# Row counts of DMA transfers in a long convolution: 52 to 50, whole to 100 and 28, and 117 and 11 to whole

## The chip, the cores and the metric

The kernel runs on one core of a Trainium2 chip. The metric is the device time of one execution in microseconds (us). The engines are TensorE (PE; PEld are its weight loads), VectorE (DVE), ScalarE (ACT), GpSimd (POOL) and SyncE (SP), which only issues DMAs. ACT issues some DMAs too. All transfers run on the core's 16 DMA engines.

## The reference

A causal convolution over the sequence by FFT, followed by a gated projection. x is 8 x 6400 x 128, h is 6400 x 128, all float32.

```
def _attn_ref(x, h):                       # S = 6400, L = 2 * S
    Xf = np.fft.rfft(x, n=L, axis=1)
    Hf = np.fft.rfft(h, n=L, axis=0)
    y = np.fft.irfft(Xf * Hf[None, :, :], n=L, axis=1)[:, :S, :]

def _moe_ref(x, w_val, conv_w, w_out):     # x is y of above, K = 5
    for k in range(K):
        gate_pre += conv_w[k][None, None, :] * xp[:, k:k + S, :]
    gate = 1.0 / (1.0 + np.exp(-gate_pre))
    return gate * (x @ w_val) @ w_out
```

## The kernel before, in words

The sequence is factored as 100 x 64 (N1, N2), and the transform goes through TensorE in four stages, each a set of matmuls with constant tables.

- **Stage 1** (`Forward`): an x tile holds 4 channels of both halves; `load` brings it in as two half tiles of 52 rows (constant TR; 50 of the rows, HR, are used by the matmuls), at partitions 0 and 64. The first three tiles of each batch (and the first eight of the kernel) come as one transfer of 128 rows. `sums` makes sums and differences (tile sd), `half` does the 16 matmuls per tile and half, and two ACT copies write gy.
- **Stage 2** (`Product`): 13 blocks, each with a table block of m2 (128 rows of 4,096 bytes) and a block of the spectrum of h, hd. Both come into a ring: three m2 places and four hd places, 4,096 bytes a row each.
- **Stage 3** (`s3_quads`): 16 steps g per batch. A step does a quad of stage 3 on PE, and in the same step stage 1 of the next batch (`fx.half`, `fx.sums`, which also loads the next x tile), the loads of ring blocks for the coming stage 2 (`ahead`, issued by ACT, by the table AHEAD of step to block), and for chunks of the batch the value projection, gating, output projection and store (tables VALUE and OUTPUT of chunk to step; nine chunks are stored in stage 3). In the first batch, steps 0 to 7 also load pieces of the table m4 (`m4_load`).
- **Stage 4** (`s4`, `copies`, `taps`): interleaved with stage 2 of the next batch.

The **head** is stage 1 of h and of the first x, then stage 2 of both together. Its first six m2 blocks come through `spread`, which cuts a transfer at row KR = 117 into one of 117 rows and one of 11.

The order on every engine is the program's order (`_InOrder`). SP issues DMAs in that order, and stands at one whose semaphores are not there yet; so does ACT. The DMAs of SP and ACT together use eight completion semaphores (DMAHW0 to 7) in turn.

Everything is issued by one wrapper, so that all instructions of the profile have line L122; groups are told apart by their tiles: x (x tiles), sd, gy and gh (stage 1 out), pt (PSUM), ring (the ring, and stage 4 values that live in it), m_sb (table m4, and in the head x tiles and m2 blocks that use its place), yl, gl, p (stage 4), xl, hl, m, hd, out (DRAM).

Of the kernel before, what the change touches and what calls it, by code (L numbers as in the profile page):

```python
# [16 lines left out]
C = 128  # L17
# [3 lines left out]
HR = N1 // 2  # L21
HP = 64
MW = 3 * HR
M4H = 4
SB = 4
# [14 lines left out]
M2B = 3  # L40
MH = 6
HB = 4
XB = 3
XH = 8
TR = 52
M2_AT = (14, 19, 24, 27, 29)
KR = 117
VALUE = {10: 0, 15: 1, 20: 2, 25: 4, 30: 5, 35: 6, 40: 8, 45: 10, 50: 12, 55: 14}
OUTPUT = {10: 2, 15: 3, 20: 4, 25: 6, 30: 7, 35: 8, 40: 9, 45: 11, 50: 13}
ORDER = (60, 0, 35, 40, 45, 50, 55, 5, 10, 25, 15, 20, 30)  # L50
KEEP = {0: 1, 5: 3, 10: 1, 15: 2, 20: 3}
AHEAD = {
    2: (1, 0, 0), 3: (1, 0, 1), 4: (0, 0, 0), 5: (0, 0, 1), 7: (1, 1, 0), 8: (0, 1, 0),
    9: (0, 1, 1), 10: (0, 2, 0), 11: (0, 2, 1), 12: (1, 1, 1), 13: (1, 2, 0), 14: (1, 2, 1),
}

# [78 lines left out]
def longconv_moe(ctx: ExitStack, tc: tile.TileContext, x, h, r1, m2, r3, m4, w64, out):  # L135
    nc = _Engines(tc)
# [15 lines left out]
    m4_sb = cp.tile([128, N2 + 2, MW], F32, name="m4_sb")  # L152
# [8 lines left out]
    m2_sb = [r.rearrange("p (s a c) -> p s a c", a=2, c=C) for r in ring_at[:M2B]]  # L161
    h_sb = [ring_at[M2B + i] for i in (2, 0, 1, 3)]
# [10 lines left out]
    hd = dp.tile([NKB, 128, 2 * SB * C], F32, name="hd")  # L173
# [74 lines left out]
    class Forward:  # L248
# [6 lines left out]
        def load(self, n=1):  # L255
            whole = len(self.xs) == XH and self.o == 0
            for _ in range(n):
                if self.n < NS:
                    t, v = self.xs[self.n % len(self.xs)], self.src[self.n]
                    if whole and self.n < XH or n > 1:  # L260
                        nc.sync.dma_start(t, v)
                    else:
                        for r in (0, HP):
                            nc.sync.dma_start(t[r : r + TR], v[r : r + TR])
                    self.n += 1

        def sums(self, e, sub=nc.gpsimd):
# [32 lines left out]
    def count(kb):  # L300
        return min(SB, HR - kb * SB)

    m4_flat = m4_sb.rearrange("p n t -> p (n t)")
    m2_head = m2_sb + [
        m4_flat[:, i * 2 * SB * C : (i + 1) * 2 * SB * C].rearrange("p (s a c) -> p s a c", a=2, c=C)
        for i in range(M2B, MH)
    ]

    def m2_load(kb, ms=m2_sb, dma=nc.sync.dma_start):
        if kb < NKB:  # L310
            n = count(kb)
            dma(ms[kb % len(ms)][:, :n], m2[:, kb * SB : kb * SB + n])

    def h_load(kb):
        if kb < NKB:
# [1 line left out]
            nc.sync.dma_start(h_sb[kb % HB][:, :n], hd[kb, :, :n])  # L317

    def ahead(spectrum, kb, half):
        i = half * SB // 2  # L320
        if spectrum:
            k = slice(2 * C * i, 2 * C * i + SB * C)
            nc.scalar.dma_start(h_sb[kb % HB][:, k], hd[kb, :, k])
        else:
            j = kb * SB + i
            nc.scalar.dma_start(m2_sb[kb % M2B][:, i : i + SB // 2], m2[:, j : j + SB // 2])

    def laid(t, kb):
        n = count(kb)
# [22 lines left out]
    class Spectrum:  # L352
# [7 lines left out]
        def store(self):  # L360
            n = 2 * count(self.kb) * C
            nc.sync.dma_start(hd[self.kb, :, :n], self.h[:, :n])
# [83 lines left out]
    class Chunk:  # L446
# [119 lines left out]
                        self.o[k * HP : (k + 1) * HP, i : i + o.shape[1]], lhsT=w, rhs=o, start=True, stop=True  # L566
                    )

        def store(self, y=None):
            y = self.y if y is None else y  # L570
            act(y, self.o)
            i, k = _out_range(self.ch)
            nc.sync.dma_start(out[self.b, i:k].rearrange("(e n t) -> e n t", e=C, n=self.ch[1]), y)

# [14 lines left out]
    for g, (f, i) in enumerate(order):  # L591
        e = f.half()
        if g + 2 < 2 * NS:
            order[g + 2][0].sums(nc.vector, nc.vector)
        if g in M2_AT:
            m2_load(M2_AT.index(g), m2_head, spread)
        if NS - len(xh) <= g < NS:
            fx.load()
        e[0](act)
        e[1](act)  # L600
    next(wgen)
    for kb in range(len(M2_AT), MH):
        m2_load(kb, m2_head, spread)
    nc.sync.dma_start(r3_sb, r3)

    def m4_load(j, half=None):
        a = CH * j, CH * j + CH + (j == 12)
        if half is not None:
            a = (a[0] + 2 * half, a[1] if half else a[0] + 2)
        a = slice(*a)  # L610
        nc.sync.dma_start(m4_sb[:, a], m4.rearrange("k (n t) -> k n t", t=MW)[:, a])

    m4_rest = [12, 7, 5, 8, 4, 9, 10, 11, 6]
    sp, pr = {0: Spectrum(0)}, {}
# [25 lines left out]
    for b in range(B):  # L640
        nxt = b + 1 < B


        steps = collections.defaultdict(list)
        for c in pend:
            a = c.ch[0]
            if a == HEAD[0]:
                t = NS - 1
            else:
                t = VALUE[a]  # L650
            if c.late:
                k = (a - WAIT) // CH
                if not nxt:
                    c.r = rows[k % 3]
                steps[2 * k] += [lambda c=c: c.taps(range(2))]
                steps[2 * k + 1] += [lambda c=c: c.taps(range(2, 4)), c.add]
            steps[t] += [c.project]
            steps[t if a in OUTPUT else NS - 1] += [c.sigm, c.gate]
            if a in OUTPUT:
                steps[OUTPUT[a]] += [c.output]  # L660
                steps[OUTPUT[a] + 1] += [c.store]
        pend = [c for c in pend if c.ch[0] in (HEAD[0], HEAD[0] - CH)]
        for g in range(NS):
            e = s3_quads(4 * g)
            f = []
            if nxt:
                f = fx.half([single(), single()])
                fx.sums(nc.gpsimd)
            for u in e:
                u()  # L670
            if nxt and g in AHEAD:
                ahead(*AHEAD[g])
            for u in f:
                u(act)
            if b == 0:
                next(wgen, None)
                next(wgen, None)
                if g < 8:
                    m4_load(m4_rest[0], g % 2)
                    if g % 2:  # L680
                        m4_rest.pop(0)
            for u in steps[g]:
                u()
        if nxt:
            h_load(HB - 1)
        if b + 2 < B:
            fx = Forward(x[b + 2], gy)


        chs = CHUNKS if not nxt else [(a, CH) if a < HEAD[0] else HEAD for a in ORDER]  # L690
        cs = [Chunk(b, i, ch, nxt) for i, ch in enumerate(chs)]
        jobs = collections.defaultdict(list)
        for i, c in enumerate(cs):
            if i and not c.late and not c.held:
                jobs[i + 3].append(c)
        if not nxt:
            jobs[NCH + 2].append(cs[0])
        pr = {}

        def s2(kb):  # L700
            if nxt and kb < NKB:
                pr[kb] = Product(kb)
                m2_load(kb + M2B)

        def times(kb):
            if kb in pr:
                pr[kb].mul_u()
                pr[kb].mul_t()
                pr.pop(kb).add()
                h_load(kb + HB)  # L710

        outs, at = [], 0
        for s in range(max(NCH, *jobs) + 2):
            kbs = list(range(at, min(at + 2 - s % 2, NKB))) if nxt else []
            at += len(kbs)
            if s == 0:
                s2(0)
                s2(1)
            if s < 2:
                cs[s].s4()  # L720
            late = pend[s : s + 1]
            if late and s == 0:
                late[0].output()
            for kb in kbs[:1]:
                if kb:
                    s2(kb + 1)
            if m4_rest:
                m4_load(m4_rest.pop(0))
            for c in jobs[s]:
                c.project()  # L730
            if 1 < s < NCH:
                cs[s].s4()
            for c in outs + late[: s]:
                c.output()
            for c in jobs[s]:
                c.sigm()
            for kb in kbs[:1]:
                times(kb)
            for kb in kbs[1:]:
                s2(kb + 1)  # L740
            if s < NCH:
                cs[s].copies()
            for c in outs + late:
                c.store(p_t[0][:, : c.ch[1]] if s == 0 or nxt and c.ch[0] == CH else None)
            for kb in kbs[1:]:
                times(kb)
            if 0 < s <= NCH and not cs[s - 1].late:
                cs[s - 1].taps()
            for c in cs[1:]:
                if not c.late and s == c.i + (3 if c.held and c.ch[0] == HELD else 2):  # L750
                    c.add()
            for c in jobs[s]:
                c.gate()
            outs = jobs[s]
            if b + 2 < B:
                if s == 5:
                    fx.load(XB)
                if s in (10, 11):
                    fx.sums(nc.gpsimd)
        pend = [cs[0]] + [c for c in cs if c.held or c.late]  # L760
# [45 lines left out]
```

## Time and profile before

| | us |
|---|---|
| median of 3 runs | 935.6 |
| lowest, highest | 933.1, 936.11 |
| profiled execution | 933.86 |
| its span, first to last instruction | 932.0 |
| PE busy | 855.5 |
| DVE busy | 744.5 |
| POOL busy | 560.4 |
| ACT busy | 515.7 |

The profile is of one execution, whose own time of 933.86 us stands beside its span; 1.86 us lie around the span. Busy times are of engines that work side by side, so they don't add up. A wait is idle time of an engine ahead of an instruction, put down to the event that ended it.

The span falls into the head's stage 1 (0 to 45 us), its stage 2 (45 to 95), the third stage of the first batch (95 to 145), then in turn stages 4 and 2 (some 52 us) and stage 3 (some 54 us) of each further batch, and the last batch's end from 832 us on.

### The profile page before, as it was taken

To read this page: it belongs to the slowest core of one execution; us is meant where nothing else is said; L and a number is where in the kernel's file an instruction comes from. 1 tells how busy PE (TensorE), PEld (TensorE's weight loads), DVE (VectorE), ACT (ScalarE), POOL (GpSimd) and SP (SyncE) were. 2 spreads that over 40 slices of the span, in tenths; PEclk is the share of its full clock that TensorE was granted. 3 is DMA by queue.
4 is the path that set the end of the run, shared out by engine and by line. 5 is a ranking of instruction groups with operands and counts; after the bars stand their busy time and mean duration, and the time that the engine had idled before them with its cause. 6 is when DMAs were issued, how large, how long until landed. Compare 5 with 4: busy or idle time off the path is not lost. (4 is left out here: it accounts for less than half of the span.)

```text
span 932.0 us, 48248 instructions
## 1 busy us (share of the span) xinstructions
PE 855.5 (92%) x21360; PEld 683.5 (73%) x21360; DVE 744.5 (80%) x1057; ACT 515.7 (55%) x1238; POOL 560.4 (60%) x570
## 2 busy tenths in 40 slices
PE   6799668999999999999999999999999989999897
PEld 6699668965699558976689567985689657984563
DVE  5456657888887978888797978888897887978786
ACT  6532452277624874177623875167723785258776
POOL 0046644786477864877477855877558763765333
PEclk9899889999999999999999999999999999999999
DMA  7786647926594456925585465925586364921112
GB/s 241 228 294 225 188 140 238 339 67 185 171 312 154 147 175 204 317 70 172 164 298 180 127 189 171 329 87 167 176 275 223 107 181 159 326 78 48 67 57 99
DMA packets 77847, 171.80 MB, mean 184 GB/s; under 512 B 15246, under 2 KB 28558, under 8 KB 77638
## 3 DMA queue, kind: packets, MB, share of 16 engines
q1 hardware_dynamic: 65542, 146.68, 47.0%
q10 hardware_dynamic: 12096, 22.03, 8.2%
q8 instruction: 168, 2.75, 1.3%
q14 instruction: 41, 0.34, 0.1%
HBM read 135.90 MB, written 32.77 MB: 181 GB/s over the span
## 5 line engine op out<-in xcount | busy, mean ns | idle before, releaser
L122 POOL TENSOR_TENSOR gy<-gy,ring 128x512 f32<-128x512 f32 (+1 forms) x182 | 220.4, 1240 | 103.9 <-DVE ring L122 52.6
L122 PEld LDWEIGHTS pt<-r_sb,gy 64*64 64x64 f32 x8192 | 143.2, 138 | 108.1 <-issue 73.9
L122 PEld LDWEIGHTS pt<-m_sb,dt 128*64 128x64 f32 x4096 | 184.8, 136 | 24.0 <-issue 10.6
L122 DVE TENSOR_TENSOR dt<-pt,ring 128x496 f32<-128x496 f32 x256 | 159.6, 665 | 47.2 <-ACT dt L122 45.9
L122 PE MATMUL pt<-m_sb,dt 128*64 128x100 f32 x4096 | 191.4, 248 | 4.3 <-DVE ring L122 2.9
L122 PE MATMUL pt<-gy,ring 128*64 128x128 f32 x3008 | 187.6, 278 | 8.2 <-PE pt L122 3.1
L122 ACT COPY ring<-pt 128x512 f32<-128x512 f32 (+2 forms) x216 | 128.2, 601 | 116.6 <-PE pt L122 48.8
L122 POOL TENSOR_TENSOR sd<-x 128x256 f32<-128x256 f32 x224 | 179.6, 831 | 17.9 <-issue 13.3
L122 PEld LDWEIGHTS pt<-gy,ring 128*64 128x64 f32 x3008 | 174.7, 135 | 20.3 <-PE pt L122 8.0
L122 PE MATMUL pt<-r_sb,gy 64*64 64x64 f32 x8192 | 162.6, 226 | 19.9 <-issue 14.2
L122 PE MATMUL pt<-r_sb,sd 50*64 50x100 f32 x4608 | 141.0, 260 | 25.7 <-issue 18.6
L122 DVE TENSOR_TENSOR gy<-pt,ring 128x1024 f32<-128x1024 f32 (+1 forms) x99 | 117.0, 1182 | 55.5 <-PE pt L122 53.7
L122 PEld LDWEIGHTS pt<-r_sb,sd 50*64 50x64 f32 x4608 | 119.0, 142 | 31.8 <-issue 21.9
L122 DVE TENSOR_TENSOR ring<-pt,ring 128x1024 f32<-128x1024 f32 (+2 forms) x131 | 134.6, 1027 | 7.0
L122 ACT COPY gy<-pt 128x400 f32<-128x400 f32 x256 | 113.5, 503 | 30.8 <-PE pt L122 24.9
L122 ACT COPY yl<-pt 128x500 f32<-128x500 f32 (+1 forms) x89 | 51.2, 575 | 125.9 <-PE pt L122 125.8
L122 POOL TENSOR_TENSOR gl<-gl,p 128x500 f32<-128x500 f32 (+1 forms) x46 | 54.1, 1177 | 101.9 <-DVE gl L122 50.8
L122 ACT COPY dt<-pt 128x16 f32<-128x16 f32 (+3 forms) x318 | 65.3, 265 | 67.5 <-PE pt L122 67.5
L122 DVE SCALAR_TENSOR_TENSOR gl<-yl,w_sb,gl 128x500 f32<-128x500 f32 (+1 forms) x107 | 94.1, 884 | 3.3 <-ACT gl L122 1.2
L122 PE MATMUL pt<-ring,w_sb 128*64 128x500 f32 x320 | 82.6, 602 | 10.0 <-DVE ring L122 9.2
L122 DVE SCALAR_TENSOR_TENSOR ring<-pt,w_sb,ring 128x500 f32<-128x500 f32 (+3 forms) x94 | 63.2, 672 | 11.8 <-ACT ring L122 7.4
L122 POOL TENSOR_TENSOR gy<-gy,m_sb 128x512 f32<-128x512 f32 x24 | 30.4, 1286 | 65.4 <-DVE m_sb L122 65.4
(59 smaller groups left out, 765.7 us busy)
## 6 DMA issues: line engine op xcount, KB each, us to landing
ring<-m SPq DMA_DIRECT2D x66, 512.0 KB
ring<-hd SPq DMA_DIRECT2D x63, 512.0 KB
x<-xl SPq DMA_DIRECT2D x194, 104.0 KB
ring<-hd ACTq DMA_DIRECT2D x42, 256.0 KB
ring<-m ACTq DMA_DIRECT2D x42, 256.0 KB
out<-ring SPq DMA_DIRECT2D x40, 250.0 KB
out<-yl SPq DMA_DIRECT2D x40, 250.0 KB
x<-xl SPq DMA_DIRECT2D x21, 256.0 KB
```

Source lines behind the costliest of these rows:

```text
L122: return self._tc.keep_in_program_order(call(*args, **kwargs))
```

## The change: row counts of transfers

- x half tiles have 50 rows (HR) instead of 52.
- `spread` now cuts at row 100 (KR), into 100 and 28 rows. It is used for the nine stores of a third stage and for the pieces of m4 in the first batch's third stage, which were transfers of 128 rows.
- The ring blocks that ACT loads in stage 3 were two halves by columns (128 rows of 2,048 bytes); now they are 100 and 28 rows of 4,096 bytes. The two loads of m2 block 0 move from steps 4 and 5 to 5 and 6.
- The head's six m2 blocks come in one transfer of 128 rows each.

```diff
-TR = 52
-KR = 117
+KR = 100
 AHEAD = {
-    2: (1, 0, 0), 3: (1, 0, 1), 4: (0, 0, 0), 5: (0, 0, 1), 7: (1, 1, 0), 8: (0, 1, 0),
+    2: (1, 0, 0), 3: (1, 0, 1), 5: (0, 0, 0), 6: (0, 0, 1), 7: (1, 1, 0), 8: (0, 1, 0),
...
                         for r in (0, HP):
-                            nc.sync.dma_start(t[r : r + TR], v[r : r + TR])
+                            nc.sync.dma_start(t[r : r + HR], v[r : r + HR])
...
     def ahead(spectrum, kb, half):
-        i = half * SB // 2
+        r = slice(KR, 128) if half else slice(0, KR)
         if spectrum:
-            k = slice(2 * C * i, 2 * C * i + SB * C)
-            nc.scalar.dma_start(h_sb[kb % HB][:, k], hd[kb, :, k])
+            nc.scalar.dma_start(h_sb[kb % HB][r], hd[kb, r])
         else:
-            j = kb * SB + i
-            nc.scalar.dma_start(m2_sb[kb % M2B][:, i : i + SB // 2], m2[:, j : j + SB // 2])
+            nc.scalar.dma_start(m2_sb[kb % M2B][r], m2[r, kb * SB : kb * SB + SB])
...
         if g in M2_AT:
-            m2_load(M2_AT.index(g), m2_head, spread)
+            m2_load(M2_AT.index(g), m2_head)
...
-                steps[OUTPUT[a] + 1] += [c.store]
+                steps[OUTPUT[a] + 1] += [lambda c=c: c.store(dma=spread)]
...
-                    m4_load(m4_rest[0], g % 2)
+                    m4_load(m4_rest[0], g % 2, spread)
```

The instructions of PE, DVE and POOL stand in the same order as before; only DMA rows differ.

On SP, in the third stage of the second batch, where x half tiles and outputs alternate (in brackets the semaphores waited for: DMAHW are earlier DMAs, Pool is GpSimd's sums, Activation the copy that makes the output), before:

```order
L122 DMA x_83<-xl 52x512 [waits DMAHW2_49,Pool_49]
L122 DMA x_83<-xl 52x512 [waits DMAHW3_49]
L122 DMA out<-ring 128x500 [waits DMAHW4_49,Activation_49]
L122 DMA x_81<-xl 52x512 [waits DMAHW5_49,Pool_49]
L122 DMA x_81<-xl 52x512 [waits DMAHW6_49]
L122 DMA out<-ring 128x500 [waits DMAHW0_49,DVE_49,Activation_49]
L122 DMA x_82<-xl 52x512 [waits DMAHW1_49,Pool_49]
```

and now:

```order
L121 DMA x_83<-xl 50x512 [waits DMAHW4_49,Pool_49]
L121 DMA x_83<-xl 50x512 [waits DMAHW5_49]
L121 DMA out<-ring 100x500 [waits DMAHW6_49,Activation_49]
L121 DMA out<-ring 28x500 [waits DMAHW7_49]
L121 DMA x_81<-xl 50x512 [waits DMAHW0_49,Pool_49]
L121 DMA x_81<-xl 50x512 [waits DMAHW1_49]
L121 DMA out<-ring 100x500 [waits DMAHW2_49,DVE_49,Activation_49]
L121 DMA out<-ring 28x500 [waits DMAHW3_49]
L121 DMA x_82<-xl 50x512 [waits DMAHW5_49,Pool_49]
```

Each output is two transfers, the x half tiles keep their place, and the eight semaphores come round sooner.

On ACT, in the third stage of the first batch, steps 3 to 5 (the copies feed gy, which stage 2 of the next batch reads), before:

```order
L122 DMA ring<-hd 128x512 [waits DMAHW3_49]
L122 COPY gy<-pt_1592 128x400 [waits PE_49]
L122 COPY gy<-pt_1593 128x400
L122 COPY ring<-pt_1625 128x32x2x8 [waits DVE_49,PE_49,Activation_49]
L122 COPY dt<-pt_1625 128x4x4 x2
L122 DMA ring<-m 128x512 [waits DMAHW7_49,DMAHW0_49]
L122 COPY gy<-pt_1658 128x400 [waits PE_49]
L122 COPY gy<-pt_1659 128x400
```

and now:

```order
L121 DMA ring<-hd 28x1024 [waits DMAHW6_49]
L121 COPY gy<-pt_1589 128x400 [waits PE_49]
L121 COPY gy<-pt_1590 128x400
L121 COPY ring<-pt_1623 128x32x2x8 [waits DVE_49,PE_49,Activation_49]
L121 COPY dt<-pt_1623 128x4x4 x2
L121 COPY gy<-pt_1656 128x400 [waits PE_49]
L121 COPY gy<-pt_1657 128x400
L121 COPY ring<-pt_1689 128x32x2x8 [waits DVE_49,PE_49,Activation_49]
L121 COPY dt<-pt_1689 128x4x4 x2
L121 DMA ring<-m 100x1024 [waits DMAHW2_49]
```

The ring loads stand between the same copies, the first m2 load one step later, and each still waits for an earlier DMA's semaphore.

## Rows read from the trace of the kernel before

**Rows 1.** The page: busy us, share, instructions of PE, PEld and others.

```profile
PE 855.5 (92%) x21360; PEld 683.5 (73%) x21360; DVE 744.5 (80%) x1057; ACT 515.7 (55%) x1238; POOL 560.4 (60%) x570
```

**Rows 2.** Windows: length, busy (xcount) PE PEld DVE ACT POOL, clock, DMA share, GB/s.

```profile
0.00:45.00 45.00, 31.76 (x1026) 30.03 (x1026) 23.37 (x65) 27.26 (x63) 0.20 (x4) 0.90 0.77 239
95.00:145.00 50.00, 34.33 (x1536) 32.38 (x1536) 29.61 (x56) 25.15 (x80) 24.38 (x33) 0.87 0.51 155
...
196.00:250.00 54.00, 50.31 (x1622) 31.87 (x1618) 47.08 (x69) 42.15 (x115) 37.06 (x41) 1.00 0.52 159
250.00:302.00 52.00, 50.70 (x951) 47.26 (x954) 44.34 (x57) 18.16 (x36) 35.80 (x34) 1.00 0.68 227
```

**Rows 3.** PE's issue waits (us, times, longest): span, 0:45, 95:145, 196:250, 726:780.

```profile
PE pt L122 <- issue: 32.9, 32, 2.8
...
PE pt L122 <- issue: 8.5, 6, 2.8
...
PE pt L122 <- issue: 13.7, 9, 2.3
...
PE pt L122 <- issue: 1.0, 2, 0.7
...
PE pt L122 <- issue: 2.0, 2, 1.7
```

**Rows 4.** Timeline of PE, head: start, us, instruction, xcount, idle before.

```profile
16.40 2.97 PE L122 MATMUL pt<-r_sb,sd 50*64 50x100 f32 x126 [0.23 <-issue]
21.45 4.62 PE L122 MATMUL pt<-r_sb,sd 50*64 50x100 f32 x126 [2.08 <-issue]
26.55 2.97 PE L122 MATMUL pt<-r_sb,sd 50*64 50x100 f32 x126 [0.49 <-issue]
31.35 4.61 PE L122 MATMUL pt<-r_sb,sd 50*64 50x100 f32 x126 [1.83 <-issue]
```

**Rows 5.** Timeline of PE, third stage of the first batch.

```profile
134.04 0.83 PE L122 MATMUL pt<-r_sb,gy 64*64 64x64 f32 x40 [1.75 <-issue]
...
137.76 0.39 PE L122 MATMUL pt<-r_sb,gy 64*64 64x64 f32 x9 [1.37 <-issue]
...
141.95 0.47 PE L122 MATMUL pt<-r_sb,sd 50*64 50x100 f32 x10 [1.66 <-issue]
```

**Rows 6.** The page's DMA queues: packets, MB, share of 16 engines.

```profile
q8 instruction: 168, 2.75, 1.3%
```

**Rows 7.** DMA queues and issues in 194.3 to 198.5 us.

```profile
q1 hardware_dynamic: 274, 0.47, 32.7%
...
out<-p SPq DMA_DIRECT2D x1, 250.0 KB
x<-xl SPq DMA_DIRECT2D x2, 104.0 KB
```

**Rows 8.** DMA queues in 0:45 (one row), 95:145 and 196:250.

```profile
q1 hardware_dynamic: 5454, 10.61, 75.3%
...
q1 hardware_dynamic: 2842, 4.38, 28.5%
q10 hardware_dynamic: 1728, 3.15, 20.9%
q8 instruction: 12, 0.20, 1.6%
...
q1 hardware_dynamic: 3084, 5.24, 29.0%
q10 hardware_dynamic: 1728, 3.15, 21.0%
```

**Rows 9.** Timeline of SP, one output's issue.

```profile
215.96 0.37 SPq L122 DMA_DIRECT2D out<-ring  x1
```

**Rows 10.** SP's waits in 196 to 250: us in total, times, longest.

```profile
SPq L122 <- POOL sd L122: 23.1, 10, 3.6
```

**Rows 11.** Timeline of ACT, third stage of the first batch.

```profile
107.84 0.33 ACTq L122 DMA_DIRECT2D ring<-hd  x1
108.20 0.89 ACT L122 COPY gy<-pt 128x400 f32<-128x400 f32 x2 [1.95 <-DMA m_sb<-m]
```

More of the change, by code (lines that the diff above doesn't have):

```diff
@@ L307, in longconv_moe, with m2_load @@
     ]
-    def m2_load(kb, ms=m2_sb, dma=nc.sync.dma_start):
+    def m2_load(kb, ms=m2_sb):
         if kb < NKB:
             n = count(kb)
-            dma(ms[kb % len(ms)][:, :n], m2[:, kb * SB : kb * SB + n])
+            nc.sync.dma_start(ms[kb % len(ms)][:, :n], m2[:, kb * SB : kb * SB + n])
     def h_load(kb):
@@ L567, in output, with store @@
                     )
-        def store(self, y=None):
+        def store(self, y=None, dma=nc.sync.dma_start):
             y = self.y if y is None else y
@@ L572, in store @@
             i, k = _out_range(self.ch)
-            nc.sync.dma_start(out[self.b, i:k].rearrange("(e n t) -> e n t", e=C, n=self.ch[1]), y)
+            dma(out[self.b, i:k].rearrange("(e n t) -> e n t", e=C, n=self.ch[1]), y)
     wgen = weights()
@@ L602, in longconv_moe, with m4_load @@
     for kb in range(len(M2_AT), MH):
-        m2_load(kb, m2_head, spread)
+        m2_load(kb, m2_head)
     nc.sync.dma_start(r3_sb, r3)
-    def m4_load(j, half=None):
+    def m4_load(j, half=None, dma=nc.sync.dma_start):
         a = CH * j, CH * j + CH + (j == 12)
@@ L610, in m4_load @@
         a = slice(*a)
-        nc.sync.dma_start(m4_sb[:, a], m4.rearrange("k (n t) -> k n t", t=MW)[:, a])
+        dma(m4_sb[:, a], m4.rearrange("k (n t) -> k n t", t=MW)[:, a])
     m4_rest = [12, 7, 5, 8, 4, 9, 10, 11, 6]
```

## The prediction

> **What bounds the kernel now.** I read the share of each engine first: TensorE (PE) is busy 92% of the span [rows 1]. The stretches by stage then say where the missing 8% lies. The second and fourth stage of a batch (250 to 302 us) have PE busy 50.70 of 52 us, the third stage of a steady batch (196 to 250) 50.31 of 54, but the head (0 to 45) 31.76 of 45, and the third stage of the first batch (95 to 145) 34.33 of 50 [rows 2]. So PE is the bound almost everywhere, and two places of some 50 us each are bound by something else.
>
> The waits of PE name it badly: 32.9 us are put down to "issue", 8.5 of them in the head and 13.7 in 95 to 145 [rows 3]; the other 10.7 us lie in the six steady third stages (windows of 54 us from 196 us on, every 106 us), 1.0 us in the first and 2.0 in the last. Issue means that PE waited for nothing the profile shows. The timeline shows what it is. In the head PE starts again at 16.40, 21.45, 26.55 and 31.35 us, each time for exactly 126 matmuls [rows 4]. 126 matmuls and 126 weight loads are 252 instructions. The page counts 168 packets of queue 8, kind "instruction", with 2.75 MB, 16.4 kB each [rows 6], and PE with its weight loads has 42,720 instructions [rows 1]: 254 to a packet. So PE runs through one packet of instructions and stands until the next has come. That the fetch and not the work sets the pace is seen in the spacing: 5.05, 5.10 and 4.80 us, whether the 126 matmuls took 2.97 or 4.62 us (the granted clock of the head is 0.90 in the mean, so part of it ran at 1.2 GHz) [rows 2, 4]. In the first batch's third stage, with less DMA traffic (155 against 239 GB/s), PE starts again at 134.04, 137.76 and 141.95: 3.72 and 4.19 us apart [rows 2, 5]. The same packet comes 1.0 us sooner (3.96 against 4.98 in the mean). So a fetch gets later when the DMA engines are busier, and what this change does to the time, it does by the load on the DMA engines that these fetches run on.
>
> **How a transfer lies on the engines.** In 194.3 to 198.5 us only two x half tiles of 52 rows and one output of 128 rows run, and queue 1 moved 274 packets [rows 7]. 2 x 52 + 128 = 232 are rows; the 42 left are completions, 13 for each x half tile and 16 for the output. 128 is divisible by 16, and 52 by 13 but not by 14, 15 or 16. I take it that a transfer runs on as many engines as the largest divisor of its row count up to 16: 50 rows on 10, 100 on 10, 28 on 14, 117 on 13, 11 on 11. Which engines these are no row tells. If always the same ones, engines 0 to 9 get nearly everything in the changed third stage; if another ten each time, the load stays even. The Trainium skill (DMA: Bandwidth & Descriptors, section Why a DMA increments its semaphore by 16 and not by 1) says that transfers of these two queues take the lowest-numbered ones; by it the first case holds throughout. No row decides it: I take the first for the sum, as the case in which the change moves load at all, and the second is part of the second rival.
>
> **The load, part by part.** Price of a byte: in 95 to 145 both queues took 28.5% and 20.9% of 16 engines' 50 us for 4.38 + 3.15 MB, 52 ns a kB; in 196 to 250 it is 51.5, in 0 to 45 51 [rows 8].
>
> Third stage, first batch. x: 26 half tiles of 52 rows of 2,048 B, 2.77 MB; table pieces 1.61 MB (the rest of queue 1); ring blocks 3.15 MB. Before, engines 0 to 12 move 2.77/13 + 4.76/16 = 0.51 MB, 26.6 us of 50 (53%), and 13 to 15 0.30 MB (31%). After, x is 2.66 MB on ten engines, and of the rest 78% on ten and 22% on fourteen: engines 0 to 9 move 0.266 + 0.372 + 0.074 = 0.71 MB, 37 us (74%), 10 to 13 0.07 MB (8%), 14 and 15 nothing. In a steady batch (outputs, 2.30 MB, for table pieces) the same working gives 54% before and 75% after on the loaded ones, 33% (13 to 15) before and 9% or less (10 to 15) after.
>
> What a fetch waits for, as an estimate: half of one step's work on its engine, times the share in which the engine is busy. A steady stage has 16 steps, so 29 us of load are 1.8 us a step: 0.54 x 0.9 = 0.49 us before, 0.75 x 1.27 = 0.95 after; on 13 to 15 before 0.19, on the six free ones after about nothing. A fetch on a loaded engine loses 0.46 us; one on an engine that becomes free gains at most 0.49. The two spacings give a second price: 1.0 us between a share of 89% (head, below) and 53%, so 0.6 us for the step from 53% to 75%. Fetches I take as spread evenly over the 16 engines.
>
> - **First batch's third stage:** queue 8 has 12 fetches there [rows 8], and nearly all bind. Mean wait before 13/16 x 0.49 + 3/16 x 0.19 = 0.43, after 10/16 x 0.95 = 0.60; 12 x 0.17 = **+2 us**. Bounds: -5.1 (six of sixteen parts of the 13.7 us vanish, no loss elsewhere) and +4.5 (12 x 10/16 x 0.6, no gain).
> - **Six steady third stages:** 72 fetches, 45 on loaded engines. If all of these bind, 45 x 0.46 = 20.7 us; if none that now comes in time turns late, about nothing. PE is within 4 us of full there, so there is little slack; I take half, 10 us. The gain can be no more than the stalls that are there: 6/16 x 10.7 = 4 us. **+6 us**, bounds -4 and +20.7. This lopsidedness is the argument: a fetch that comes sooner than needed is worth nothing, one that comes later stops PE.
> - **Head:** 48 x half tiles (5.11 MB) and six table blocks (3.15 MB) of 10.61 MB [rows 8]. Before, engines 0 to 10 move 0.393 + 0.246 + 0.147 = 0.79 MB, 40 of 45 us (89%), 13 to 15 17%. After, blocks lie on all sixteen: 0 to 9 0.83 MB (95%), 10 to 15 39%. Six or seven fetches: about 0.5 us more on ten engines, 1 us less on three. **0**, bounds -3 and +3. The six issues saved stand on a queue that waits.
> - **Issues:** 65 more on SP (63 outputs and 8 table pieces twice, 6 blocks once less), at 0.37 us each [rows 9]. In 196 to 250 SP waits 23.1 us for GpSimd's sums [rows 10], which hides them: 0. x tiles, 5 packets deep instead of 4, come 0.1 us later, with three buffers: 0. If that cover were gone, each of the 54 split steady outputs would hold the x issue behind it 0.37 us.
> - **Completion slots:** all DMAs of SP and ACT share eight semaphores in program order, so each issue waits for the eighth DMA before it. Two transfers per output and table piece use them up faster: 3.3 a step becomes 3.9 in a steady batch, 3.8 becomes 4.8 in the first. ACT waits with its next copy of gy behind its ring load. That happened once: ACT stood 1.95 us before the gy copy at 108.20, released by a table piece's landing, with its ring issue at 107.84 in between [rows 11]. **+2 us**, bounds 0 and +6 (three such waits).
> - **Ring blocks** wait for the whole block instead of half its columns; two loads stand one step later for it. The last load is still issued two steps before the stage ends: 0.
>
> Sum +10 us, against the profiled execution's 933.86: 944. That execution is 1.7 us under the median, so **945 us**.
>
> **Rivals.** A change under 0.3% (2.8 us) is about what a measurement of this kernel cannot tell from none.
>
> 1. *Six engines freed are worth more than ten loaded ones cost.* Place: the third stages. If a fetch on a loaded engine waits no longer than now (it is let in between packets), and fetches on the six others come at once, 6/16 of the 13.7 and 10.7 us go: 9 us, 925 to 927. It decides where the loss on a loaded engine is under 0.6 of the gain on a free one. For it: the free engines do exist after the change. Against it: in the head engines 13 to 15 are nearly free now, and the stalls are longest there.
> 2. *Nothing measurable*: loads are even after all, or the fetch's place on its engine does not depend on the load. Then the mean load falls by 4% of x alone: 934 to 936. The Trainium skill (DMA: Bandwidth & Descriptors, section Queues, rings and completion order) says that an engine takes turns between its queues packet by packet; by it a fetch waits for a packet or two, 0.1 us each, on whatever engine, and this rival holds. The two spacings, 4.98 and 3.96 us, are what speaks against it.
> 3. *More than the sum:* the fetches run on the loaded engines alone, or ACT waits at most of its ring loads (12 in each of seven third stages). All 72 steady fetches x 0.46 with half of them binding are 16.6, the 12 of the first batch 5.5, slots 6: +28, 962.
>
> **Chances.** Forecast 0.52, rival 3 0.12, both slower: 0.64. Rival 2 0.19: same. Rival 1 0.17: faster. Reaching down into rival 1 and up into rival 3 until 2 in 10 are left out, the range is 930 to 960; of the slower cases alone it is 939 to 962.
>
> **What would show it.** Right: the issue waits of PE grow in the steady third stages from some 1.8 to 3 us each, at 256-instruction spacing; second and fourth stages keep their length; the head stays within 3 us; queue 1's completions fall to 10 for each x half tile. Wrong: third stages of steady batches shorter than 54 us with fewer issue waits (rival 1), or the same waits (rival 2). ACT's waits for DMAs above 6 us in sum would show the slots as the larger part (rival 3). An x tile that arrives late (GpSimd waiting for x) would be a cause that I count as nothing.

## The result: 943.44 us, slower by 1.2 per cent

The changed kernel takes 943.44 us (median of 4 runs, 942.56 to 955.22) against 934.35 us (4 runs, 931.2 to 936.11) of the kernel before beside it: a ratio of 1.0125 [1.0082, 1.0168]. In a second comparison (experiment g1 below) it is 946.94 against 936.85 us, 1.0100 [1.0069, 1.0131]. The profiled execution took 942.58 us with a span of 940.8, 8.8 us longer than before's 932.0.

The page of the changed kernel, with the engines' shares and the queues (packets, MB, share of 16 engines):

```profile
PE 856.4 (91%) x21360; PEld 684.5 (73%) x21360; DVE 745.4 (79%) x1057; ACT 515.6 (55%) x1238; POOL 557.8 (59%) x570
...
q1 hardware_dynamic: 64912, 145.74, 47.0%
q10 hardware_dynamic: 6384, 22.02, 7.5%
q8 instruction: 168, 2.75, 1.2%
```

PE does the same work in the same busy time (855.5 us before [rows 1]), and as many instruction packets are fetched [rows 6]. The granted clock is 0.984 in the mean of this execution and 0.985 in before's, so it is not the cause. So 7.9 of the 8.8 us are idle time of PE. Where they lie is read from ACT's timeline: its first ring load of each third stage (step 2) and its last (step 14) are marks that both kernels have. The columns are start, us, engine, instruction. The kernel before, first batch, second batch and the first mark of the last:

```profile
103.06 0.35 ACTq L122 DMA_DIRECT2D ring<-hd  x1
...
140.24 0.33 ACTq L122 DMA_DIRECT2D ring<-hd  x1
...
203.13 0.34 ACTq L122 DMA_DIRECT2D ring<-hd  x1
...
245.66 0.33 ACTq L122 DMA_DIRECT2D ring<-hd  x1
...
735.17 0.33 ACTq L122 DMA_DIRECT2D ring<-hd  x1
```

and the changed kernel:

```profile
104.09 0.55 ACTq L121 DMA_DIRECT2D ring<-hd  x1
...
144.11 0.31 ACTq L121 DMA_DIRECT2D ring<-hd  x1
...
207.26 0.28 ACTq L121 DMA_DIRECT2D ring<-hd  x1
...
250.49 0.31 ACTq L121 DMA_DIRECT2D ring<-hd  x1
...
745.44 0.28 ACTq L121 DMA_DIRECT2D ring<-hd  x1
```

Up to the first mark 1.0 us were lost; from there to the second batch's mark 3.1 us (103.17 against 100.07), of which 2.8 lie between the two marks of the first batch's third stage (40.02 against 37.18); over the next five batches 6.1 us (538.18 against 532.04); and behind the last mark 1.5 us were won (195.36 against 196.83). Taken in the same way, the six steady third stages last 258.64 us in sum before and 261.07 after; in g1, a second execution of the changed kernel, 263.93. The marks leave out a stage's first two steps and its last. From the first to the last of PE's stage 3 matmuls (`r_sb,gy`), the first batch's third stage takes 51.25 us in place of 48.25 and the six steady ones 322.26 in place of 318.25: 7.0 of the 8.8 us, and 11.6 of 12.6 in g1. So most of the loss lies in the third stages, as forecast. It is the waits that are not the forecast ones. The chain of waits of the changed kernel over the span (us in total, times, longest):

```profile
DVE gl L121 <- ACT gl L121: 38.7, 29, 3.1
...
PEld pt L121 <- DVE gl L121: 28.5, 42, 1.4
...
PE pt L121 <- issue: 27.1, 28, 2.5
...
ACT gy L121 <- DMA out<-ring: 15.7, 11, 2.2
...
PE pt L121 <- DVE gl L121: 11.1, 18, 1.6
...
ACT gy L121 <- DMA m_sb<-m: 3.1, 1, 3.1
...
ACT gy L121 <- DMA x<-xl: 2.1, 1, 2.1
```

and the same waits of the kernel before that the front does not show:

```profile
DVE gl L122 <- ACT gl L122: 18.7, 22, 2.3
...
PEld pt L122 <- DVE gl L122: 14.8, 20, 1.4
...
PE pt L122 <- DVE gl L122: 4.8, 4, 1.5
...
ACT gy L122 <- DMA m_sb<-m: 2.0, 1, 2.0
...
ACT gy L122 <- DMA out<-ring: 1.4, 1, 1.4
...
ACT gy L122 <- DMA x<-xl: 0.8, 1, 0.8
```

PE's issue waits were to grow. They are 27.1 us after 32.9 [rows 3], and 32.0 in g1; two executions of one kernel differ by nearly as much, so a fall is not shown, but a growth is not there. From the second batch's third stage on (from 196 us before, from 200 us now), where the forecast put the growth, they are, before and now (9.2 in g1):

```profile
PE pt L122 <- issue: 10.7, 17, 1.7
...
PE pt L121 <- issue: 6.3, 15, 0.7
```

ACT's waits for DMAs went from 4.2 to 20.9 us, 15.7 of it for outputs, eleven times. Behind ACT stands DVE (18.7 to 38.7), and behind DVE stands PE (4.8 to 11.1, its weight loads 14.8 to 28.5). That is the largest growth of a wait of PE, not the only one: its waits for DVE's sd go from 4.8 to 7.6 us, for table blocks of the ring from 1.2 to 2.8, for GpSimd's sd from 0.3 to 1.7. One case of the chain in the second batch's third stage of the changed kernel, in the timeline (in brackets the idle time before and what ended it):

```profile
220.43 0.68 SPq L121 DMA_DIRECT2D out<-ring  x2
...
224.93 0.33 ACTq L121 DMA_DIRECT2D ring<-m  x1
225.29 0.89 ACT L121 COPY gy<-pt 128x400 f32<-128x400 f32 x2 [1.47 <-DMA out<-ring]
...
226.07 0.63 ACT L121 ACTIVATE gl<-gl 128x500 f32<-128x500 f32 x1
...
226.74 0.68 DVE L121 TENSOR_TENSOR gl<-pt,gl 128x500 f32<-128x500 f32 x1 [1.63 <-ACT gl L121]
...
227.34 1.51 DVE L121 SCALAR_TENSOR_TENSOR gl<-yl,w_sb,gl 128x500 f32<-128x500 f32 x2
227.47 0.20 PEld L121 LDWEIGHTS pt<-ring,w_sb 128*64 128x64 f32 x4 [0.36 <-DVE gl L121]
227.47 1.06 PE L121 MATMUL pt<-ring,w_sb 128*64 128x500 f32 x4 [0.17 <-DVE gl L121]
```

ACT has nothing to do with the output but issues its ring load in order, and that load is not issued before the DMA eight issues earlier, whose semaphore it takes over, has landed (its last completion has come). ACT is idle or issuing for the 1.47 us before 225.29, then copies gy, then makes the factor of gl that DVE waits for, and DVE makes what PE waits for. Of ACT's 1.47 us PE feels little in this case: it stands for 0.17 us, and its weight loads for 0.36. The trace has the semaphore number of every DMA. The load at 224.93 has number 102; so has the first of the two outputs issued at 220.43, the part of 100 rows, and its last completion is at 224.91. It took 4.5 us to land.

### The profile page after: what moved, and what is told of

Same layout as the page of the kernel before. It is cut to its first block, busy times and chain, and to the rows that moved or that the text cites. A ratio compares the mean times of both kernels' runs of the same rounds, so it can differ in the third digit from the quotient of the medians.

```text
span 940.8 us, 48341 instructions
## 1 busy us (share of the span) xinstructions
PE 856.4 (91%) x21360; PEld 684.5 (73%) x21360; DVE 745.4 (79%) x1057; ACT 515.6 (55%) x1238; POOL 557.8 (59%) x570
## 2 busy tenths in 40 slices
DMA packets 71506, 170.86 MB, mean 182 GB/s; under 512 B 14740, under 2 KB 28052, under 8 KB 71296
## 3 DMA queue, kind: packets, MB, share of 16 engines
q10 hardware_dynamic: 6384, 22.02, 7.5%
## 5 line engine op out<-in xcount | busy, mean ns | idle before, releaser
L121 PEld LDWEIGHTS pt<-m_sb,dt 128*64 128x64 f32 x4096 | 184.8, 136 | 24.0 <-issue 10.7
L121 POOL TENSOR_TENSOR sd<-x 128x256 f32<-128x256 f32 x224 | 176.7, 818 | 23.2 <-PE pt L121 12.3
L121 PE MATMUL pt<-r_sb,gy 64*64 64x64 f32 x8192 | 162.3, 227 | 20.6 <-issue 14.2
```

The source lines that it names most:

```text
L121: return self._tc.keep_in_program_order(call(*args, **kwargs))
```

## The experiments

Two theories at first. **S (slots):** outputs and pieces in two transfers use the eight completion semaphores up sooner, so ACT stands at its ring loads. **L (load):** engines 0 to 9 carry too much, so that instruction fetches and x come late; ACT's waits are a sign, not the cause. After the first four kernels, two others. **P (product):** ACT's standing costs much only where rows of the ring and of the outputs are cut together. **A (additive):** each part costs its own share. Each ratio is against runs of the kernel before on the same chip.

| kernel | differs from the changed kernel | ratio, 95% interval | ACT's waits for DMAs, us (for outputs) | of these in the steady third stages |
|---|---|---|---|---|
| before | | 1 | 4.2 (1.4) | 2.2 |
| first comparison | | 1.0125 [1.0082, 1.0168] | 20.9 (15.7) | 15.7 |
| g1 | the same again | 1.0100 [1.0069, 1.0131] | 19.9 (13.8) | 13.8 |
| g4 | ring at 64 and 64 rows | 1.0090 [1.0061, 1.0120] | 18.7 (12.1) | 12.1 |
| e4 | outputs, pieces at 64 and 64 rows | 1.0046 [1.0020, 1.0071] | 15.8 (8.7) | 9.1 |
| e1 | outputs, pieces whole | 1.0030 [1.0006, 1.0054] | 8.1 (0) | 5.5 |
| e3 | ring by columns, old steps | 1.0004 [0.9979, 1.0030] | 18.6 (4.7) | 9.6 |
| e5 | ring loads issued by SP | 1.0155 [1.0114, 1.0196] | 0 | 0 |
| | **one or two parts on the kernel before** | | | |
| f1 | ring rows | 1.0015 [0.9996, 1.0034] | 7.7 (0) | 2.7 |
| f2 | output and piece rows | 0.9955 [0.9936, 0.9974] | 3.5 (0) | 1.4 |
| f3 | x in 50 rows | 0.9957 [0.9933, 0.9980] | 3.4 (0) | 2.1 |
| f4 | x in 50 rows, head blocks whole | 0.9984 [0.9954, 1.0014] | 4.9 (0) | 1.6 |
| g2 | ring rows, output and piece rows | 1.0037 [1.0011, 1.0063] | 18.5 (14.2) | 14.2 |
| g3 | x in 50 rows, output and piece rows | 1.0001 [0.9974, 1.0029] | 16.5 (4.0) | 8.2 |

The waits are of one traced execution of each kernel. Those in the first batch's third stage (1.3 to 9.0 us) do not go with the time. Those in the steady ones do, e5 aside: 12 to 16 us in the changed kernel, g1, g2 and g4 (1.0037 to 1.0125), 5 to 10 us in e1, e3, e4 and g3 (1.0001 to 1.0046), under 3 us in the others (0.9955 to 1.0015).

**e1: outputs and pieces whole again.**

```diff
-                steps[OUTPUT[a] + 1] += [lambda c=c: c.store(dma=spread)]
+                steps[OUTPUT[a] + 1] += [c.store]
...
-                    m4_load(m4_rest[0], g % 2, spread)
+                    m4_load(m4_rest[0], g % 2)
```

> The changed kernel with the third stage's outputs and table pieces in one transfer of 128 rows again; x in 50 rows and ring blocks in 100 and 28 rows stay. Theory S (slots: ACT stands at its ring loads until the eighth DMA before has landed, 15.7 us behind outputs in the changed kernel's profile): these waits of ACT fall below 4 us in sum and the time goes back to 0.995 to 1.000 of the kernel before, 930 to 934 us, with PE's issue waits as low as after the change (27 us or less). Theory L (load: PE's fetches and the x tiles come late on the ten loaded engines): load of engines 0 to 9 falls from 75% to some 65%, so about half of the 9 us is left, 938 to 940 us.

937.67 us, 1.0030: most of the loss is gone, and with it ACT's waits for outputs, as S has it; the time lies between what S and L had. PE's issue waits are 28.0 us, within what two executions of the changed kernel show (27.1 and 32.0).

**e4: the cut at 64 rows in place of 100.**

```diff
-        for r in (slice(0, KR), slice(KR, 128)):
+        for r in (slice(0, 64), slice(64, 128)):
```

> The changed kernel with outputs and table pieces cut into 64 and 64 rows instead of 100 and 28: as many DMAs, in the same places, each on all sixteen engines. Theory S: ACT still finds the eighth DMA before under way, its waits for outputs stay at two thirds or more of 15.7 us, and the time at 940 to 944 us. Theory L: the ten engines lose what the cut put on them, and the time goes to 934 to 938 us.

940.23 us, 1.0046. As many transfers and as many slots, and yet more than half of the loss goes: S as a count of transfers alone does not hold. L had a lower time still (934 to 938). How long a part of 100 rows is under way matters too: at the two ring loads that stand behind outputs (step 6 and step 10, see g4), the part in front takes 4.6 and 3.6 us to land in the mean, against 4.9 and 4.0 in the changed kernel, and the waits for outputs nearly halve (8.7 us).

**e5: ring loads moved from ACT to SP.**

```diff
-            nc.scalar.dma_start(h_sb[kb % HB][r], hd[kb, r])
+            nc.sync.dma_start(h_sb[kb % HB][r], hd[kb, r])
...
-            nc.scalar.dma_start(m2_sb[kb % M2B][r], m2[r, kb * SB : kb * SB + SB])
+            nc.sync.dma_start(m2_sb[kb % M2B][r], m2[r, kb * SB : kb * SB + SB])
```

> The changed kernel with the ring loads of the third stage issued by SP instead of ACT, in the same place of the program; rows, load on the engines and number of DMAs stay. Theory S: ACT has no DMA wait left before its gy copies, and 934 to 938 us are left; SP waits in its stead, which GpSimd's sums hide. Theory L: 942 to 945 us as with the whole change.

950.2 us, 1.0155: slower still. ACT waits for no DMA, but its waits for issue and PE's grow, and SP stands in ACT's place. PE and ACT in the chain of waits:

```profile
ACT ring L121 <- issue: 52.8, 29, 3.4
PE pt L121 <- issue: 45.5, 35, 3.7
```

and SP's own waits (the DMA queue's):

```profile
SPq L121 <- DMA x<-xl: 25.0, 13, 4.2
SPq L121 <- DMA ring<-m: 16.8, 11, 2.3
SPq L121 <- DMA out<-ring: 12.8, 14, 2.1
```

All of it now lies on queue 1 (71,296 packets, 53.9% of the engines' span). Moving the load changes where x and the blocks stand in line as well, so this kernel takes ACT's wait away only to make others; both forecasts missed, and it decides neither S nor L. Why the issue waits grow by 18 us here was not found out.

**e3: ring blocks by columns again, at the old steps.**

```diff
-    2: (1, 0, 0), 3: (1, 0, 1), 5: (0, 0, 0), 6: (0, 0, 1), 7: (1, 1, 0), 8: (0, 1, 0),
+    2: (1, 0, 0), 3: (1, 0, 1), 4: (0, 0, 0), 5: (0, 0, 1), 7: (1, 1, 0), 8: (0, 1, 0),
...
-        r = slice(KR, 128) if half else slice(0, KR)
+        i = half * SB // 2
...
-            nc.scalar.dma_start(h_sb[kb % HB][r], hd[kb, r])
+            k = slice(2 * C * i, 2 * C * i + SB * C)
+            nc.scalar.dma_start(h_sb[kb % HB][:, k], hd[kb, :, k])
```

(the table's block likewise)

> The changed kernel with the ring blocks in column halves of 128 rows again, at the steps of before; x in 50 rows, outputs and table pieces in 100 and 28 rows stay. Theory S: as many DMAs as with the whole change, so ACT's waits for outputs stay near 15 us and the time at 940 to 944 us. Theory L: 18 of some 48 kB a step on engines 0 to 9 become 12, a good third of the added load: 938 to 941 us.

936.76 us, 1.0004: undoing the ring's cut, and with it the later step of two loads, takes the whole loss back, though the outputs are still in two transfers. Neither S nor L had that. ACT still waits, for x now:

```profile
ACT gy L121 <- DMA x<-xl: 10.4, 8, 3.3
...
ACT gy L121 <- DMA out<-ring: 4.7, 2, 2.6
```

18.6 us of ACT's waits at the kernel before's time: not every wait of ACT reaches PE. 9.0 of them lie in the first batch's third stage, which is as long as before's (37.27 us between the marks, 37.18 before). In this kernel DVE waits 26.0 us for ACT's gl (38.7 in the changed one) and PE 8.6 for DVE's (11.1).

**f1: the ring's rows alone on the kernel before** (the lines of e3's diff the other way round).

> The kernel before with the ring blocks alone in 100 and 28 rows (x stays 52 rows, outputs and table pieces whole, head blocks 117 and 11). Theory P (a product: ACT stands at its ring loads only where the outputs are cut too and the ring's blocks lie in front of them on the same engines): +1 us, 0 to 2.5, and no wait of ACT for an output above 3 us in sum. Theory A (each part costs its own share of the loss): +4 to +6 us.

938.77 us, 1.0015, and no wait of ACT for an output, as P has it; A wanted 4 to 6 us.

**f2: the outputs' and pieces' rows alone** (on the kernel before, the lines of e1's diff the other way round, cut at 100).

> The kernel before with outputs and table pieces alone in 100 and 28 rows (ring blocks stay halves of the columns, x 52 rows, head blocks 117 and 11). Theory P: +1 to +3 us, ACT's waits for outputs 2 to 6 us. Theory A: +4 to +6 us.

934.18 us, 0.9955: faster, which neither theory expected. Its page has 66,110 packets on queue 1 against before's 65,542: 568 more, 8 for each of the 63 outputs and 8 pieces, which is 10 + 14 completions in place of 16. So the count of engines by the row count was right:

```profile
q1 hardware_dynamic: 66110, 146.69, 48.7%
q10 hardware_dynamic: 12096, 22.03, 8.0%
```

**f3: x in 50 rows alone.**

```diff
-                            nc.sync.dma_start(t[r : r + TR], v[r : r + TR])
+                            nc.sync.dma_start(t[r : r + HR], v[r : r + HR])
```

> The kernel before with x alone in 50 rows. If the shorter instruction fetches of the changed kernel come from the engines that x leaves free: -2 to -6 us, and PE's issue waits at 27 to 29 us instead of 32.9. If x in 50 rows gives nothing (the fetches gain from the other cuts): -0.5 to +0.5 us and issue waits of 32 to 34 us.

934.45 us, 0.9957. The time falls, the issue waits do not (31.9 us): the gain is not the six free engines' sooner fetches that were expected here. Whence it comes was not found.

**f4: x in 50 rows and the head's blocks whole.**

```diff
-            m2_load(M2_AT.index(g), m2_head, spread)
+            m2_load(M2_AT.index(g), m2_head)
...
-        m2_load(kb, m2_head, spread)
+        m2_load(kb, m2_head)
```

(with f3's)

> The kernel before with x in 50 rows and the head's table blocks in one transfer each, nothing else: the whole change without the cuts into 100 and 28 rows. If the head's part is worth nothing, the same time as with x alone in 50 rows, to 1 us. If the long transfers of 117 rows held fetches back in the head, 1 to 4 us less than that. Theory P and A alike: this is the fastest of the four.

937.06 us, 0.9984, issue waits 34.2 us. Against f3 the head's blocks cost 2.6 us, but the intervals overlap, so neither a loss nor a small gain is shown.

**g1: the changed kernel again.**

> The changed kernel itself again, in more runs, beside the kernel before. Theories P and A both rest on its 1.25 per cent, which came from four runs of each: if that holds, a ratio of 1.009 to 1.015. If some of it was the scatter of single runs (about 3 us), 1.003 to 1.008, and then the parts measured singly (+0.15 for the ring, -0.45 for outputs and pieces, -0.16 for x and the head's blocks) leave less for a joint effect, though still some, as their sum is -0.46 per cent.

1.0100: the loss is there, about 1 per cent.

**g2: ring rows and output rows together on the kernel before** (f1 and f2).

> The kernel before with the ring blocks and the outputs and table pieces in 100 and 28 rows (x 52 rows, head blocks 117 and 11). Theory P (the loss is joint between ring rows and output rows): +0.7 to +1.3 per cent, ACT waiting for outputs at its ring loads for 8 to 16 us. Theory A (each part its own share): -0.3 per cent, the sum of the two measured singly, and waits for outputs under 4 us.

940.69 us, 1.0037, where the two measured singly add up to -0.30 per cent: 0.67 per cent, or 6 us, come from their meeting. ACT's waits are those of the changed kernel:

```profile
DVE gl L122 <- ACT gl L122: 42.9, 32, 3.0
...
ACT gy L122 <- DMA out<-ring: 14.2, 9, 2.6
```

A falls. Of P the mark is right (8 to 16 us of waits) and the size is not: half of what it wanted. The changed kernel differs from this one by x in 50 rows and the head alone, so these have part in the rest.

**g3: x rows and output rows together** (f2 and f3).

> The kernel before with x in 50 rows and the outputs and table pieces in 100 and 28 rows; the ring's blocks and the head's stay. Theory A: -0.9 per cent, the sum of the two measured singly, and faster than both kernels. Theory P: the same, unless there is a joint effect of these two as well; then -0.4 per cent or less of a gain.

937.45 us, 1.0001. Each alone gives 0.43 to 0.45 per cent, both together nothing. The order of DMAs is that of f2, so here it is the landing times that change: in the steady third stages an x half tile lands after 3.3 us in the mean (3.0 in f3, 3.1 in f2), an output's part of 100 rows after 4.4 (4.0 in f2). That two cuts meet on the same ten engines would fit it and is not shown. Again ACT stands, here for x:

```profile
ACT gy L122 <- DMA x<-xl: 8.7, 7, 2.9
...
ACT gy L122 <- DMA out<-ring: 4.0, 2, 2.4
```

**g4: the ring's rows at 64 and 64.**

```diff
-        r = slice(KR, 128) if half else slice(0, KR)
+        r = slice(64, 128) if half else slice(0, 64)
```

> The changed kernel with the ring's blocks cut at 64 rows instead of 100 (two transfers each as before, of one size); outputs and pieces stay 100 and 28. If the ring's load on ten engines is what makes the outputs late (P): +0.2 to +0.6 per cent against the kernel before, ACT's waits for outputs under 9 us. If it is the cut by rows, or its place in the order of the steps, at whatever sizes: the time of the changed kernel, and waits of 12 to 18 us.

945.24 us, 1.0090, and 12.1 us of waits for outputs: the second case that its expectation names. The concentration of the ring's load on ten engines is not what matters, since parts of 64 rows lie on all sixteen (6,720 packets on queue 10: 64 rows and 16 completions for each of 84 loads). It is that the blocks are cut by rows, or that two loads stand one step later. No kernel here has one without the other, but the semaphore numbers in the traces tell whose landing each ring load waits for. In the changed kernel all waits for outputs come at two of a stage's twelve ring loads: 9.0 us at the second load of m2 block 0 (step 6) and 6.7 us at the first of block 2 (step 10). For the second load of block 0, in all six steady third stages alike:

| kernels | ring loads of block 0 | outputs | the DMA eight back | ACT's waits there, us |
|---|---|---|---|---|
| changed, g1, g2, e4, g4 | by rows, steps 5 and 6 | two parts | an output's first part | 9.0, 7.2, 9.3, 7.6, 3.8 |
| e1, f1 | by rows, steps 5 and 6 | whole | a half tile of x | 5.5, 2.7 |
| e3, f2, g3 | by columns, steps 4 and 5 | two parts | a ring load | 0 |

e3 issues as many DMAs as the changed kernel, so it is the step that decides which DMA is eight back, not the length of the rows. Nor do outputs land later in the changed kernel: a part of 100 rows takes 4.4 us in the mean of the steady third stages, 4.6 in e3. So this part of the meeting of ring and outputs is one of order. What the length of the rows costs beside it was not tried apart. A row is 4,096 bytes in place of 2,048, so that queue 10 moves the same 22.02 MB in 6,384 packets instead of 12,096. The Trainium skill (DMA: Bandwidth & Descriptors, section Queues, rings and completion order) says that an engine takes turns between its queues packet by packet. Its packet is typically a group of some 9 to 17 descriptors (single pieces of a transfer), while the profile counts every row and completion, so neither a longer turn here nor the 0.1 us of rival 2 can be read from it. No run here shows the turns.

## Why the prediction came out right, and where it did not

The time was forecast at 945 us, +10, and is +8.8 in the spans of the profiled executions and +9.1 in the medians; the sign and the place (third stages) are right. The sum got there with two wrong terms that offset each other, so that the number came this near is luck.

- **How a transfer lies on the engines:** right as far as the count goes. 568 more completions in f2, and on queue 10 42 pairs of 2 x 144 packets before and 100 + 10 + 28 + 14 after (12,096 and 6,384). That the same engines are taken each time, no run shows directly; that e4 halves the loss and that x and outputs hinder each other in g3 fits it, that g4 gives next to nothing back does not.
- **Six steady third stages, +6 by late fetches:** this is the step that failed. "The issue waits of PE grow in the steady third stages" is wrong: there they are 6.3 us (9.2 in g1) after 10.7, over the span 27.1 (32.0) after 32.9. The stages grew nevertheless, by 4.0 us from their first to their last matmul (7.2 in g1), with waits of PE behind DVE behind ACT. As far as the runs show it, the term of the slots is paid there.
- **Completion slots, +2, bounds 0 and 6:** the mechanism was right and the size too small. It was sized by one case of before [rows 11]; ACT stands for 20.9 us instead of 4.2. The prediction's own sign ("above 6 us in sum would show the slots as the larger part") came true. What it missed is that the wait has two factors: which DMA is eight back, and how long that one takes. e4 changes the second alone and gives back more than half. e3 changes the first, for one of the two loads that wait, together with the length of the ring's rows, and gives back the whole.
- **Ring blocks, 0:** right alone (f1, 1.0015), wrong in company: with the outputs cut they cost 0.8 per cent (g2 against f2), with everything else changed 1.0 (g1 against e3). The prediction names that "two loads stand one step later for it" and puts it at nothing. With the outputs in two parts, the later step puts one of these loads eight behind an output, and ACT stands there for 9.0 of the 15.7 us that it waits for outputs. PE's own waits for a table block grow by 1.6 us.
- **Issues, 0:** right. f2 has all 71 of the additional ones and is faster.
- **x in 50 rows, 0 by its delay:** a gain of 0.43 per cent alone (f3), lost again as soon as outputs are cut (g3). In the steady third stages of the changed kernel a half tile lands after 3.6 us in the mean, 3.0 before: 0.6 later, not 0.1.
- **First batch's third stage, +2:** 2.8 us between the marks, but with 13.4 us of issue waits against 13.7 [rows 3]; not the fetches. ACT stands there 3.1 us for a table piece and 2.1 for x. This stage differs by as much from kernel to kernel without a pattern (36.7 us in e4 to 42.36 in e1), so that its 2.8 us prove little.
- **Head, 0:** 1.0 us up to the first mark; f4 against f3 puts it at 2.6 us, not clear of nothing.
- **Rival 1** was right that issue waits would not grow, and wrong that this decides; **rival 3** named ACT's ring loads, at a price (28 us) that is not there.

What stays open: how much of the time the later step costs by itself and how much the length of the ring's rows, why g2 with the same waits of ACT loses less than half as much as g1, where the gain of f2 and f3 comes from (4 us each, near what single runs differ by, which is why only medians of 12 runs show it), and what holds PE back in e5. No kernel here beats before by more than f2 and f3 do alone.

## What to carry to other kernels

Where an engine that computes also issues DMAs, price each issue by the landing time of the DMA whose completion semaphore it takes over, and follow that engine's next products to the bound engine; which DMA that is has to be counted again after every edit that adds an issue or moves one, and a wait that costs nothing alone becomes real when a second edit puts a slower DMA there. Test the parts of such a change in pairs, not only singly: here two gains of 0.4 per cent gave nothing together, and a loss of 0.15 and a gain of 0.45 gave a loss of 0.4. A count of waits under one name (issue) is no measure of the time when other waits can cover it.

## What the runs showed that was not expected

Splitting each 128-row output into 100 and 28 rows (10 and 14 completions instead of 16) made the kernel faster (0.9955) as long as nothing else was cut so. And PE's issue waits, which the prediction reads as instruction fetches, range from 24.7 us (g2, slower than before) to 34.2 us (f4, no slower), with 45.5 in e5, the slowest: e5 aside, their sum does not follow the time. That a fetch which is late behind another wait costs nothing would explain it and was not tested.
